# One transformer layer on one core: attention jobs of 4 heads by 256 queries, denominators from pair sums, a 256-token feed-forward, and two PSUM banks shared between matmul groups and attention outputs

## The chip, the cores and the metric

The kernel runs on one core of one Trainium2 chip. The metric is the device time of one execution in microseconds (us); lower is better. A core has these engines: TensorE for matrix products (PE in the profile, with PEld for its weight loads), VectorE (DVE), ScalarE (ACT), GpSimd (POOL), and SyncE (SP), which starts the DMA transfers here. The kernel allocates its tiles on chip, in SBUF, and for what matmuls write one tensor in PSUM, of 8 banks of 128 partitions x 512 float32.

## The reference, cut to what matters

```python
B, S, D, H, F = 1, 2048, 1024, 32, 3584          # bf16; head width 32
def _A_ref(x, wqkv, wo):
    qkv = (x @ wqkv).reshape(B, S, 3, H, 32).transpose(2, 0, 3, 1, 4)
    q, k, v = qkv
    scores = einsum("bhqd,bhkd->bhqk", q, k) * 32 ** -0.5
    p = softmax(scores, axis=-1)
    o = einsum("bhqk,bhkd->bhqd", p, v)
    return o.transpose(0, 2, 1, 3).reshape(B, S, D) @ wo
def _B_ref(x, w1, b1, w2, b2):
    return gelu(x @ w1 + b1, approximate=True) @ w2 + b2     # tanh form
h   = x + _A_ref(layernorm(x), wqkv, wo)
out = h + _B_ref(layernorm(h), w1, b1, w2, b2)
```

The attention makes 32 x 2048 x 2048 exponentials. All of them are on ScalarE, as 1024 instructions of 128 x 1024 elements. The feed-forward has 28 blocks of 128 hidden features.

## The kernel before

The program first builds a list of tasks with their dependences. A list scheduler with fixed cost constants then chooses, at build time, the order of the instructions on each engine. Each engine gets its list in that order, with semaphore waits between the engines. So a change can move work between stages without any line saying so.

An attention job of before is 2 heads x 512 queries. Scores use 32-row tiles of the array. The products with V, the denominators (a product with ones) and all other matmuls that run during attention use four tiles of 32 columns side by side. I call four such matmuls one *step*.

```python
def mm(bank, lhsT, rhs, start, stop, reads, narrow, cols=(0, 512)):     # all other matmuls
    c0, c1 = cols
    if narrow:                                                           # during attention
        for j in range(4):
            ... p.matmul(psum[32*j:32*j+32, bank, c0:c1], lhsT[:, 32*j:32*j+32], rhs,
                         start=start, stop=stop, tile_position=(0, 32*j), ...)
        pe(fns, occ, reads=reads, writes=[B_ps[bank]], mode="col")
    else:                                                                # in the tail
        pe(lambda p: p.matmul(psum[:, bank, c0:c1], lhsT, rhs, ...), ..., mode="full")

# Att.qk: per unit, 2 score matmuls of 512 columns and one exponential of 128 x 1024
act(lambda a: a.activation(PT[:, s, :, :], psum[:, 2*u:2*u+2, :], ACT.Exp, bias=0.0, scale=SCALE), 1024, ...)

# Att.pv_unit: one step holds both the products with V and the denominators of one unit
for j in range(2):
    ... p.matmul(psum[32*j:32*j+32, bank, :], V[:, kt, 32*h:32*h+32], PT[:, s, j, :],
                 tile_position=(0, 32*j), ...)
for j in range(2):
    ... p.matmul(psum[64+32*j:96+32*j, bank, :], ones32[:, :], PT[:, s, j, :],
                 tile_position=(0, 64+32*j), ...)

# Att.finish: copies of 64 x 512 out of PSUM, then per pair of jobs four of these, and a product
v.reciprocal(Dsb[:, 128*k:128*k+128], Dsb[:, 128*k:128*k+128])
```

PSUM banks 0 to 5 hold scores. Bank 6 belongs to the attention outputs and bank 7 to all other matmul groups. With one bank, the next group waits until VectorE has emptied the bank: in the run before_again below, matmuls waited 35 times, 11.3 us in all, for the VectorE additions of the feed-forward that do this (waits view). The feed-forward of 512 tokens runs under the attention of the next 512 tokens. The last 512 tokens have no attention left to hide behind; that part is the *tail*, and it may use all eight banks.

The softmax here doesn't subtract the row's maximum and nothing guards it: scores larger than these inputs give would overflow.

Of the kernel before, what the change touches and what calls it, by code (L numbers as in the profile page):

```python
# [12 lines left out]
P = 128  # L13
# [14 lines left out]
class Task:  # L28
    __slots__ = ("eng", "fns", "occ", "lat", "deps", "prio", "kind", "mode", "left", "succ", "ready", "done",
                 "order", "inc", "flow", "value", "lane", "waits", "bytes", "hold")  # L30

    def __init__(self, eng, fns, occ, lat, prio, kind, mode):
        self.eng, self.fns, self.occ, self.lat = eng, fns, occ, lat
        self.prio, self.kind, self.mode = prio, kind, mode
        self.deps = set()
        self.succ = []
        self.left = 0
        self.ready = 0.0
        self.done = None
        self.order = None  # L40
        self.inc = False
        self.flow = None
        self.value = 0
        self.lane = None
        self.waits = ()
        self.bytes = 0
        self.hold = None


class Graph:  # L50
# [47 lines left out]
    def schedule(self, pick_pe, switch=0.1, dma_rate=280.0, dma_lat=2.1, dma_issue=0.06):  # L98
        for i, t in enumerate(self.tasks):
            t.left = len(t.deps)  # L100
            for d in t.deps:
                d.succ.append(t)
        ready = {e: [] for e in self.ENGS}
# [18 lines left out]
        while n < total:  # L122
# [5 lines left out]
            for e in self.ENGS:  # L128
                while free[e] <= now + 1e-9:
# [41 lines left out]
                    n += 1  # L171
                    for s in t.succ:
                        s.left -= 1
                        if s.left == 0:
                            release(s)
# [109 lines left out]
def build_kernel(nc, A_x, A_wqkv, A_wo, B_w1, B_b1, B_w2, B_b2, out):  # L285
# [5 lines left out]
    NCH = S // 512  # L291
# [13 lines left out]

    BASE, TOP = 16512, 229344

    class Area:
        def __init__(self, start):
            self.cur = start  # L310

        def take(self, shape, dtype, align=64):
# [6 lines left out]
            assert self.cur <= TOP, (shape, self.cur - TOP)  # L319
# [3 lines left out]


# [26 lines left out]
    att_lo = top.cur  # L351
    KT2, B_KT = sb(top, "KT2", [P, 16, 4, 2, P], BF, 64, 2)
    V, B_V = sb(top, "V", [P, NT, D], BF, 4 * NT)
    att_hi = top.cur
    NQ = 4
    QT2, B_QT = sb(top, "QT2", [P, NQ, 2, 512], BF, NQ)
    NPT = 7
    PT, B_PT = sb(top, "PT", [P, NPT, 2, 512], BF, NPT)
    ot_lo = Area(top.cur)
    OT, B_OT_ = sb(top, "OT", [P, 2, G, 512], BF, 2 * G, 4)  # L360
    B_OT = [B_OT_[:G], B_OT_[G:]]
    xrb, B_xrb = sb(ot_lo, "xrb", [P, 8, D], BF, 8)
    Osb, B_Osb = sb(top, "Osb", [P, 512], F32, parts=2)
    Dsb, B_Dsb_ = sb(top, "Dsb", [P, 512], F32, parts=8)
    B_Dsb = [B_Dsb_[:4], B_Dsb_[4:]]
    ph0 = Area(top.cur)
    ffn = Area(top.cur)


    xnT, B_xnTt = sb(ph0, "xnT", [P, 4, DC, 512], BF, 4, 4)  # L370
    Wall, B_W = sb(ph0, "Wall", [P, 6, DC, 512], BF, 6, 4)
    NXB = 4
    xb, B_xb = sb(ph0, "xb", [P, NXB, D], BF, NXB)
    NSG = 2
    stg, B_stg = sb(ph0, "stg", [P, NSG, 512], BF, NSG)


    hch, B_hch = sb(ffn, "hch", [P, 4, D], BF, 4)
    gT, B_gT = sb(ffn, "gT", [P, FC, 512], BF, FC)

    class Rings:


        def __init__(self, area, pfx, nw1, nw2, ngl, nos, nx, nxb):
            self.nw1, self.nw2, self.ngl, self.nos, self.nx, self.nxb = nw1, nw2, ngl, nos, nx, nxb
            self.cnt = {"w1": 0, "w2": 0, "x": 0, "xb": 0, "gl": 0, "os": 0}
            self.x, self.B_x = sb(area, pfx + "xr3", [P, self.nx, 512], BF, self.nx)
            self.w1, self.B_w1 = sb(area, pfx + "w1r", [P, nw1, DC, 256], BF, nw1)
            w2_area = Area(area.cur + 3 * 4096)
            self.w2, self.B_w2 = sb(area, pfx + "w2r", [P, nw2, 4, 512], BF, nw2)  # L390

            if nw2 == 7:
                self.xq, self.B_xq = sb(w2_area, pfx + "xq", [P, DC, 512], BF)
                self.hnT, self.B_hnT = sb(w2_area, pfx + "hnT", [P, DC, 512], BF, 1, 4)
            self.xb, self.B_xb = sb(area, pfx + "xb3", [P, self.nxb, D], BF, self.nxb)
            self.xh, self.B_xh = sb(area, pfx + "xh", [P, ngl, 512], BF, ngl)
            self.sq, self.B_sq = sb(area, pfx + "sq", [P, ngl, 512], BF, ngl)
            self.uu, self.B_uu = sb(area, pfx + "uu", [P, ngl, 512], BF, ngl)
            self.th, self.B_th = sb(area, pfx + "th", [P, ngl, 512], F32, ngl)
            self.ost, self.B_ost = sb(area, pfx + "ost", [P, nos, 512], BF, nos)  # L400

        def next(self, k, n):
            i = self.cnt[k] % n
            self.cnt[k] += 1
            return i

    R1 = Rings(ffn, "a_", 4, 7, 2, 2, 2, 2)
# [4 lines left out]

    qd = nc.dram_tensor("q_scratch", [G, NCH, P, 512], BF, kind="Internal").ap()
    xd = nc.dram_tensor("x_scratch", [3, P, DC, 512], BF, kind="Internal").ap()
    B_xd = [gr.buf() for _ in range(3)]
    B_qd = [[gr.buf() for _ in range(NCH)] for _ in range(G)]


    MM = 0.2195
    def c_dve_ps(n):  # L420
        return (120 + n) / 960.0 + 0.02
# [10 lines left out]
    def mm(bank, lhsT, rhs, start, stop, reads, narrow, cols=(0, 512)):  # L432

        c0, c1 = cols
        occ = MM * (c1 - c0) / 512.0 + 0.003
        if narrow:
            fns = []
            for j in range(4):
                fns.append(lambda p, j=j: p.matmul(psum[32 * j:32 * j + 32, bank, c0:c1], lhsT[:, 32 * j:32 * j + 32], rhs,  # L439
                                                   start=start, stop=stop, tile_position=(0, 32 * j), skip_group_check=True))  # L440
            pe(fns, occ, reads=reads, writes=[B_ps[bank]], mode="col")
        else:
            pe(lambda p: p.matmul(psum[:, bank, c0:c1], lhsT, rhs, start=start, stop=stop),  # L443
               occ, reads=reads, writes=[B_ps[bank]], mode="full")
# [18 lines left out]

# [10 lines left out]


    cnt = {"ln": 0, "x": 0, "sg": 0, "pt": 0}

    def layer_norm(tiles, prio, norm="dve"):

# [20 lines left out]
        for k, (x_ap, B_x, o_ap, B_o) in enumerate(tiles):  # L500
            eng, cost = (dve, 0.58) if norm == "dve" else (pool, 3.8)
            eng(lambda e, k=k, x_ap=x_ap, o_ap=o_ap: e.tensor_scalar(
                o_ap, x_ap, mvr[:, i + k, :], rden[:, i + k, :], ALU.subtract, ALU.mult), cost,
                reads=[B_x, B_mvr[i + k], B_rden[i + k]], writes=[B_o], prio=prio)

    def transposes(src_ap, B_src, bank, dst_ap, B_dst, evac, prio):
        for dc in range(DC):
            pe(lambda p, dc=dc: p.transpose(psb[:, bank, dc * P:(dc + 1) * P], src_ap[:, dc * P:(dc + 1) * P], ident[:]),  # L508
               0.064, reads=[B_src, B_ident], writes=[B_ps[bank]], prio=prio)
        src = psb[:, bank, :].rearrange("p (dc t) -> p dc t", dc=DC)  # L510
        if evac == "act":
            act(lambda a: a.activation(dst_ap, src, ACT.Copy), 1024, reads=[B_ps[bank]], writes=[B_dst], prio=-1)  # L512
        else:
            dve(lambda v: v.tensor_copy(dst_ap, src), c_dve_ps(1024), reads=[B_ps[bank]], writes=[B_dst])


    def load_w(blk, prio, c0=0, c1=512, after=()):
        dma(Wall[:, blk, :, c0:c1], A_wqkv[:, blk * 512 + c0:blk * 512 + c1].rearrange("(dc p) c -> p dc c", p=P),
            P * DC * (c1 - c0) * 2, writes=B_W[blk][c0 // P:c1 // P], prio=prio, after=after)

    def x_slot(tt):
        return xrb[:, tt % 8, :], B_xrb[tt % 8]
# [5 lines left out]
    def ln_tiles(tts, prio, norm):  # L528
        layer_norm([x_slot(tt) + (xb[:, tt % NXB, :], B_xb[tt % NXB]) for tt in tts], prio, norm)

    def tr_tile(tt, bank, evac, prio=0):
        tc, t4 = divmod(tt, 4)
        transposes(xb[:, tt % NXB, :], B_xb[tt % NXB], bank, xnT[:, tc, :, t4 * P:(t4 + 1) * P], B_xnTt[tc][t4], evac, prio)

    def proj(which, g, tc, bank, evac, direct=False):

        blk, c = divmod(which * D + g * P, 512)
        for dc in range(DC):
            mm(bank, Wall[:, blk, dc, c:c + P], xnT[:, tc, dc, :], dc == 0, dc == DC - 1,
               [B_W[blk][c // P]] + B_xnTt[tc], True)  # L540
        s = cnt["sg"] % NSG
        cnt["sg"] += 1
        if evac == "act":
            act(lambda a: a.activation(stg[:, s, :], psum[:, bank, :], ACT.Copy), 512,
                reads=[B_ps[bank]], writes=[B_stg[s]], prio=-1)
        else:
            dve(lambda v: v.tensor_copy(stg[:, s, :], psum[:, bank, :]), c_dve_ps(512), reads=[B_ps[bank]], writes=[B_stg[s]])  # L547
        if which == 1:
            for pr in range(2):
                for half in range(2):  # L550
                    dve(lambda v, pr=pr, half=half: v.tensor_copy(
                        KT2[64 * half:64 * half + 64, 2 * g + pr, tc, :, :],
                        stg[64 * pr:64 * pr + 64, s, 256 * half:256 * half + 256]), c_dve(256, 4),
                        reads=[B_stg[s]], writes=[B_KT[4 * (2 * g + pr) + tc][half]])
        else:
            if direct:
                for pr in range(2):
# [449 lines left out]
```

## Time and profile before

The timed runs took 1204.71 us (median; 1203.74 to 1205.07). The first profiled execution took 1417.9 us. The page of that profile, its first rows: busy time with share of the span and instruction count per engine; the granted TensorE clock in 40 slices, in tenths of full speed; the shares of the chain of work that ended last; and two groups of instructions (busy us, mean ns | idle time before them and what ended it).

```profile
span 1417.9 us, 37847 instructions
PE 1366.2 (96%) x17326; PEld 510.9 (36%) x17336; DVE 673.2 (47%) x1165; ACT 1085.3 (77%) x1189; POOL 37.9 (3%) x96
PEclk7777777777777777777777777777777777766777
PE 91%; ACT 4%; DVE 3%; issue 1%; POOL 1%; DMA 0%; POOLq 0%; DVEq 0%
L643 ACT ACTIVATE PT<-ps 128x1024 bf16<-128x1024 f32 x1024 | 989.2, 1025 | 180.5 <-PE ps L634 166.1
L673 DVE RECIPROCAL Dsb<-Dsb 128x128 f32<-128x128 f32 x128 | 115.1, 928 | 1.0
```

This page looks like a kernel bound by TensorE, but the clock row is 6 to 7 from end to end (0.749 in the mean), and the span is 18% longer than the timed runs. It is a page taken at a lower clock. There is a second run of the kernel before (label before_again, 1204.6 us). The same parts of its page, with two rows on DMA (all packets; and queue q8, which carries instructions: packets, MB, share of the engines' time):

```profile
span 1202.8 us, 37857 instructions
PE 1130.1 (94%) x17336; PEld 465.1 (39%) x17336; DVE 668.8 (56%) x1165; ACT 1059.9 (88%) x1189; POOL 38.2 (3%) x96
PEclk9999999999999999999999999999999999978999
DMA packets 165793, 112.29 MB, mean 93 GB/s; under 512 B 25345, under 2 KB 162817, under 8 KB 164866
q8 instruction: 136, 2.23, 0.8%
L643 ACT ACTIVATE PT<-ps 128x1024 bf16<-128x1024 f32 x1024 | 967.6, 1034 | 33.5 <-PE ps L634 20.1
```

And the view of windows for 100 us in the middle of attention (busy us and count of PE, PEld, DVE, ACT, POOL; clock; DMA share; GB/s):

```profile
500.00:600.00 100.00, 95.88 (x1528) 36.11 (x1520) 42.91 (x65) 99.16 (x107) 4.60 (x12) 1.00 0.35 110
```

| kernel before, at full clock | us |
|---|---|
| start to the first exponential | 23.3 |
| first to last exponential ("attention") | 1050.8 |
| of that, ScalarE idle | 34.9 |
| tail, after the last exponential | 128.7 |

### The profile page before, as it was taken

Reading aid. Unit: us, or ns where it says so; the run is one execution under the profiler, and the core shown is the slowest. Engines: PE = TensorE matmul, PEld = TensorE weight load, DVE = VectorE, ACT = ScalarE, POOL = GpSimd, SP = SyncE. Lnnn points to the kernel's source line nnn. Section 1 sums busy time; section 2 is a strip of 40 time slices with the busy share of each in tenths; the row PEclk is TensorE's granted clock in tenths of the full one; section 3 lists DMA queues with packets and bytes.
Section 4 is the critical chain, followed back from the end, with each engine's and each line's share of the span. In section 5 each row is a group of like instructions: output and inputs, shape, how many; then the busy total and the mean of one; then the engine's idle time right before and its main releaser. Section 6 shows DMA issues by size and latency. Waiting matters only on the chain.

```text
span 1417.9 us, 37847 instructions
## 1 busy us (share of the span) xinstructions
PE 1366.2 (96%) x17326; PEld 510.9 (36%) x17336; DVE 673.2 (47%) x1165; ACT 1085.3 (77%) x1189; POOL 37.9 (3%) x96
## 2 busy tenths in 40 slices
PE   8999999999999999999999999999999999978999
PEld 5544443433333333332333333333333333324333
DVE  7354444443546774223547762225677612245710
ACT  4778787878888888888888888888988888844500
POOL 2000000000100000000100000000000000001000
PEclk7777777777777777777777777777777777766777
DMA  6800000025343222303342230422323322202222
GB/s 165 224 2 13 28 13 14 13 72 156 101 122 101 76 69 72 124 16 98 107 124 71 83 98 16 124 71 63 107 73 98 102 66 85 87 0 75 74 93 71
DMA packets 165793, 112.29 MB, mean 79 GB/s; under 512 B 25345, under 2 KB 162817, under 8 KB 164866
## 3 DMA queue, kind: packets, MB, share of 16 engines
q1 hardware_dynamic: 165634, 109.87, 26.2%
q8 instruction: 136, 2.23, 0.7%
q14 instruction: 23, 0.19, 0.1%
HBM read 98.58 MB, written 11.27 MB: 77 GB/s over the span
## 4 chain that ended last, share of the span: by engine, by line
PE 91%; ACT 4%; DVE 3%; issue 1%; POOL 1%; DMA 0%; POOLq 0%; DVEq 0%
PE ps L439 48%; PE ps L654 17%; PE ps L634 12%; PE ps L443 10%; ACT PT L643 3%; PE ps L658 2%; PE ps L798 1%; ACT xnT L512 1%; DVE a_xh L748 1%; PE ps L508 1%; DVE V L606 0%; DVE stg L547 0%; DVE Osb L668 0%; DVE Dsb L666 0%; DMA a_w1r<-in_A_wqkv_dram 0%
## 5 line engine op out<-in xcount | busy, mean ns | idle before, releaser
L643 ACT ACTIVATE PT<-ps 128x1024 bf16<-128x1024 f32 x1024 | 989.2, 1025 | 180.5 <-PE ps L634 166.1
L654 PE MATMUL ps<-PT,V 128*32 128x512 bf16 x2048 | 383.4, 457 | 13.7 <-DVE V L606 6.2
L658 PE MATMUL ps<-PT,ones 128*32 128x512 bf16 x2048 | 384.8, 458 | 0.0
L439 PE MATMUL ps<-a_w2r,gT 128*32 128x512 bf16 x2688 | 241.9, 452 | 0.0
L634 PE MATMUL ps<-QT,KT 32*128 32x512 bf16 x2048 | 216.7, 414 | 7.4 <-ACT PT L643 7.3
L439 PE MATMUL ps<-a_hnT,a_w1r 128*32 128x512 bf16 x2688 | 215.2, 454 | 4.0 <-DVE a_xh L748 3.2
L654 PEld LDWEIGHTS ps<-PT,V 128*32 128x32 bf16 x2048 | 103.3, 104 | 143.9 <-issue 89.3
L634 PEld LDWEIGHTS ps<-QT,KT 32*128 32x128 bf16 x2048 | 51.5, 91 | 272.3 <-ACT PT L643 164.5
L439 PE MATMUL ps<-xnT,Wall 128*32 128x512 bf16 x1344 | 111.6, 453 | 7.0 <-ACT xnT L512 4.8
L439 PEld LDWEIGHTS ps<-a_w2r,gT 128*32 128x32 bf16 x2688 | 77.3, 109 | 112.0 <-issue 103.3
L673 DVE RECIPROCAL Dsb<-Dsb 128x128 f32<-128x128 f32 x128 | 115.1, 928 | 1.0
L439 PEld LDWEIGHTS ps<-a_hnT,a_w1r 128*32 128x32 bf16 x2688 | 70.6, 107 | 108.0 <-issue 71.4
L782 DVE SCALAR_TENSOR_TENSOR a_ost<-ps,hch 128x512 bf16<-128x512 f32 x24 | 16.6, 692 | 189.8 <-PE ps L439 189.7
L658 PEld LDWEIGHTS ps<-PT,ones 128*32 128x32 bf16 x2048 | 103.5, 104 | 6.6 <-issue 6.6
L748 DVE TENSOR_SCALAR a_xh<-ps,b1f 128x512 bf16<-128x512 f32 x84 | 63.1, 751 | 81.3 <-PE ps L439 80.2
L666 DVE COPY Dsb<-ps 64x512 f32<-64x512 f32 x64 | 44.4, 694 | 101.5 <-PE ps L658 100.1
L439 PE MATMUL ps<-Wall,xnT 128*32 128x256 bf16 x2048 | 83.8, 314 | 0.0
L547 DVE CAST stg<-ps 128x512 bf16<-128x512 f32 x40 | 27.5, 689 | 89.2 <-PE ps L439 89.2
L443 PE MATMUL ps<-a_hnT,b_w1r 128*128 128x512 bf16 x219 | 64.5, 470 | 2.1 <-ACT a_hnT L512 1.5
L439 PEld LDWEIGHTS ps<-Wall,xnT 128*32 128x32 bf16 x2048 | 57.6, 107 | 22.7 <-issue 11.3
L443 PE MATMUL ps<-a_w2r,gT 128*128 128x512 bf16 x219 | 64.1, 461 | 0.5
L439 PE MATMUL ps<-a_w1r,OT 128*32 128x512 bf16 x768 | 63.1, 453 | 0.8 <-DVE hch L719 0.5
(69 smaller groups left out, 875.5 us busy)
## 6 DMA issues: line engine op xcount, KB each, us to landing
a_w2r<-in_B_w_dram SPq DMA_DIRECT2D x56, 512.0 KB, 4.6
a_w1r<-in_B_w_dram SPq DMA_DIRECT2D x42, 512.0 KB, 3.9
a_w1r<-in_A_wo_dram SPq DMA_DIRECT2D x16, 512.0 KB, 4.7
QT<-q_scratch SPq DMA_DIRECT2D x60, 128.0 KB, 2.8
b_w1r<-in_B_w_dram SPq DMA_DIRECT2D x14, 512.0 KB, 3.8
a_w1r<-in_A_wqkv_dram SPq DMA_DIRECT2D x11, 512.0 KB, 5.1
xrb<-in_A_x_dram SPq DMA_DIRECT2D x16, 256.0 KB, 3.9
Wall<-in_A_wqkv_dram SPq DMA_DIRECT2D x16, 256.0 KB, 5.4
```

The source lines that it names most:

```text
L439: fns.append(lambda p, j=j: p.matmul(psum[32 * j:32 * j + 32, bank, c0:c1], lhsT[:, 32 * j:32 * j + 32], rhs, start=start, stop=stop, tile ...
L443: pe(lambda p: p.matmul(psum[:, bank, c0:c1], lhsT, rhs, start=start, stop=stop), occ, reads=reads, writes=[B_ps[bank]], mode="full")
L508: pe(lambda p, dc=dc: p.transpose(psb[:, bank, dc * P:(dc + 1) * P], src_ap[:, dc * P:(dc + 1) * P], ident[:]), 0.064, reads=[B_src, B_ide ...
L547: dve(lambda v: v.tensor_copy(stg[:, s, :], psum[:, bank, :]), c_dve_ps(512), reads=[B_ps[bank]], writes=[B_stg[s]])
L634: return p.matmul(psum[:, 2 * u + j, :], KT2[r0:r0 + 32, p16, tc, i, :], QT2[r0:r0 + 32, qs, pr, :], start=True, stop=True, tile_position= ...
L643: act(lambda a, u=u, s=s: a.activation(PT[:, s, :, :], psum[:, 2 * u:2 * u + 2, :], ACT.Exp, bias=0.0, scale=SCALE), 1024, reads=[B_ps[2 * ...
L654: fns.append(lambda p, j=j, h=h: p.matmul(psum[32 * j:32 * j + 32, bank, :], V[:, kt, 32 * h:32 * h + 32], PT[:, s, j, :], start=first, st ...
L658: fns.append(lambda p, j=j: p.matmul(psum[64 + 32 * j:96 + 32 * j, bank, :], ones32[:, :], PT[:, s, j, :], start=first, stop=last, tile_po ...
L666: dve(lambda v: v.tensor_copy(Dsb[64 * pr:64 * pr + 64, :], psum[64:128, bank, :]), c_dve_ps(512), reads=[B_ps[bank]], writes=B_Dsb[pr], p ...
L673: dve(lambda v, k=k: v.reciprocal(Dsb[:, 128 * k:128 * k + 128], Dsb[:, 128 * k:128 * k + 128]), 0.93, reads=[B_Dsb[0][k], B_Dsb[1][k]], w ...
L748: dve(lambda v, i=i, fc=fc, bank=bank: v.tensor_scalar(R.xh[:, i, :], psum[:, bank, :], b1f[:, fc:fc + 1], None, ALU.add), c_dve_ps(512), ...
L782: dve(lambda v, o=o, t4=t4, j=j, bank=bank: v.scalar_tensor_tensor(R.ost[:, o, :], psum[:, bank, :], 0.5, hch[:, t4, 512 * j:512 * j + 512 ...
```

## The change

The intent: fewer TensorE steps for the attention outputs, short reciprocals, a tail half as large, and no waiting for one PSUM bank.

- A job is 4 heads x 256 queries. Its products with V fill four column tiles of 256 columns. For the denominators VectorE first adds two blocks of exponentials (496 *pair sums*, all but the first two jobs), so the product with ones is needed on half the data.
- The denominators are transposed in blocks of 32 x 32, so 8 reciprocals per partition replace 128 (0.928 us).
- wo, the second layer norm and the feed-forward run in chunks of 256 tokens. Weights are read from memory eight times instead of four. All these matmuls, now in the tail too, are four column tiles of 256 columns.
- Banks 6 and 7 form a pool. The scheduler gives a free one to the next matmul group or the next job.

The core of the diff:

```diff
-    def mm(bank, lhsT, rhs, start, stop, reads, narrow, cols=(0, 512)):
+    def mm(g, lhsT, rhs, start, stop, reads, cols=(0, 512)):
         c0, c1 = cols
+        fns = []
+        for j in range(4):
+            fns.append(lambda p, j=j: p.matmul(psum[32 * j:32 * j + 32, g.bank, c0:c1], lhsT[:, 32 * j:32 * j + 32], rhs, ...))
+        grp_pe(g, fns, occ, reads, "col")
...
+    class Job:                                   # 4 heads x 256 queries; 8 rounds
+        def round(self):
...                                               # 8 score matmuls of 256 columns, 2 exponentials of 128 x 1024
+            if not self.direct:
+                dve(lambda v: v.tensor_tensor(PS[:, z, :, :], PT[:, s, :, 0:256], PT[:, s, :, 256:512], ALU.add), ...)
+            for i in range(2):
+                for hh in range(4):
+                    ... p.matmul(psum[32*hh:32*hh+32, self.bank, 0:256], V[:, g, 2*r+i, 32*hh:32*hh+32],
+                                 PT[:, s, hh, 256*i:256*i+256], tile_position=(0, 32*hh), ...)
+        def den(self, r, s):
+            srcs = [PT[:, s, :, 0:256], PT[:, s, :, 256:512]] if self.direct else [PS[:, s, :, :]]
...                                               # ones32 times each source: 4 matmuls of 256 columns
+        def finish(self):
+            v.transpose(DT[:, f, :], psum[:, self.bank, 256:512])
+            v.tensor_copy(OS[:, f, :], psum[:, self.bank, 0:256])
+            v.reciprocal(RB[:, f, :], ...)        # 8 elements per partition
+            v.transpose(RT[:, f, :], ...)
+            v.tensor_tensor(OT[:, c % NOT, g, :], OS[:, f, :], RT[:, f, :], ALU.mult)
...
     def pick_pe(rd, now, state, up):             # qk first, then pv, then the rest, as before
+        free = [b for b, ts in pool_of.items() if all(x.done is not None and x.done <= now + 1e-9 for x in ts)]
...
+            if t.grp.bank is None:                # a group takes a free bank when it starts
+                b = free[0]
+                t.grp.bank = b
+                t.deps.update(pool_of[b])
+                pool_of[b] = t.grp.buf.r
```

The static order holds 4488 steps before and 4240 after (counted in units of 512 columns), of which 525 and 383.5 follow the last scores. The number of matmul instructions rises from 17,336 to 32,304.

## The prediction

> **What bounds the kernel now.** The profiled execution took 1417.9 us, the timed ones 1204.7. The granted clock in the profile is 0.75 from 17 us on (page row PEclk). Back-to-back 512-column matmul steps (four 32-column tiles count as one) start 0.285 us apart[...]. The instruction order holds 4488 such steps: 4488 x 0.285 = 1278 us, more than the timed runs took. So the timed runs had a faster clock, and the profile's "PE 96%" is no proof for them.[...]
>
> ScalarE: 18 consecutive exponentials take 16.60 us, one per 0.916. 1024 of them, 84 tanh at about 0.53 and 16 copies need about 1000 us, all before the tail. The tail (after the last exponential at 1255 us, timeline) has no attention: 525 steps, 163 us profiled, an estimated 125 at full clock. Start 25 + tail 125 leaves 1055 us for attention; ScalarE needs 1000 of it[...]. Main reading (60%): ScalarE bounds, at full clock. Rival (40%): a clock near 0.87, TensorE bounds as in the profile.
>
> **What the change does.**
> - TensorE: PV and denominators fall from 1024 steps to about 512 + 256. Total 4488 to 4240, -5.5%. Matmuls rise from 17,300 to 32,300, most now 256 columns; in the trace 256-column steps go at 0.145 us, so halving the width costs 1 to 2% at this clock.
> - VectorE: adds 496 pair sums of 128x1024 bf16 (the 128x512 square took 0.42 us[...], so about 0.69 each, 340 us) and 64 finishes of five short operations, about 120 us. Removes reciprocals (115 us), half-bank copies (88), staging shuffles (about 60). 673 to about 920 us, over 80% of the span: a near-bound.
> - ScalarE: 98 tanh instead of 84 under attention, +7 us.
> - Tail: by the order listing 383 steps follow the last scores instead of 525: -30 us of matmul, about -5 of waits.
> - Between two score groups: 6.6 steps before, 6.4 after, but 8.6 and 7.7 in the first two sixteenths (projections), where TensorE is the slower.
>
> So most of the saved steps pay for tail work moved under attention.
>
> **Sum.** If ScalarE bounds: 1205 - 35 (tail) + 7 (tanh) + 10 (early projections) - 10 (fewer one-bank stalls) = 1177. If TensorE bounds: 1205 x 0.945 = 1138. Weighted, with some credit for pooled banks: **1158 us**, range 1105 to 1195. Chances: 0.70 / 0.24 / 0.06 (faster, same, slower).
>
> **What would show it.** Tail after the last exponential a quarter shorter (timeline). If the profile after is at 0.75 again, its span falls to about 1340, TensorE still over 90% in the chain, ScalarE's idle before exponentials under 180 us. Pair sums 0.65 to 0.72 us, VectorE at least 65% of the profiled span. TensorE's waits for VectorE evacuations under 40 us. Undoing the pair sums alone should cost under 2% if ScalarE bounds, about 5% if TensorE does.
>
> **What would make it wrong.** VectorE delaying evacuations, so that two pooled banks starve TensorE (1200 or more). 256-column steps limited by weight loads or issue at full clock[...]. Or one-bank stalls being the true loss of before: then pooling gains more, down to 1100.

The sum came to 1205 - 35 + 7 + 10 - 10 = 1177 if ScalarE bounds and 1205 x 0.945 = 1138 if TensorE does, weighted to 1158. What it says of full clock is the author's estimate; the first profile's own figures give nearly the same: 163 us x 0.75 = 122 for the tail (125 in the text), 142 fewer steps x 0.285 us x 0.75 = 30. The 0.69 us of a pair sum is an estimate (measured later: 0.684 us, and 0.420 us for half of it in a1_halfsum). The clock of that profile was 0.75 from 5.4 us on, not from 17, but for two stretches at 0.5.

## The result, and the profile after

The changed kernel took 1217.01 us (median of 4; 1213.38 to 1223.95), the kernel before 1204.24 us in the same rounds. The ratio is 1.0115 with a 95% interval of 1.0083 to 1.0146. Ratios here are the mean time of one kernel's fast runs over that of the other's fast runs in the same rounds, so they are not quite the ratio of the medians quoted. The change made the kernel 1% slower; the predicted range ended at 1195.

The page after, the rows that answer to those of before:

```profile
span 1214.9 us, 68329 instructions
PE 1107.3 (91%) x32304; PEld 775.5 (64%) x32304; DVE 836.0 (69%) x1575; ACT 1053.0 (87%) x1183; POOL 34.7 (3%) x80
PEclk9999999988999999999999999999999999998999
DMA packets 332265, 170.06 MB, mean 140 GB/s; under 512 B 26321, under 2 KB 329425, under 8 KB 331986
q8 instruction: 252, 4.13, 1.4%
PE 73%; ACT 16%; DVE 7%; issue 4%; POOL 0%; DVEq 0%; POOLq 0%; ACTq 0%
L676 ACT ACTIVATE PT<-ps 128x1024 bf16<-128x1024 f32 x1024 | 974.4, 1033 | 66.9 <-PE ps L668 53.3
L681 DVE TENSOR_TENSOR PS<-PT 128x1024 bf16<-128x1024 bf16 x496 | 328.8, 684 | 96.0 <-PE ps L705 56.4
```

The window of 500 to 600 us after:

```profile
500.00:600.00 100.00, 92.72 (x2844) 66.89 (x2844) 71.94 (x136) 93.65 (x105) 2.70 (x4) 1.00 0.59 171
```

ScalarE fell from 99.16 to 93.65 us busy in this window. TensorE did not rise in its place: it fell too, from 95.88 to 92.72. Neither engine is saturated, and the clock is 1.00. The stages, from the times of the first and last exponential in each trace:

| stage, us | before (before_again) | after | difference |
|---|---|---|---|
| to the first exponential | 23.3 | 18.9 | -4.3 |
| attention | 1050.8 | 1090.7 | +39.9 |
| of that, ScalarE idle | 34.9 | 63.1 | +28.2 |
| tail | 128.7 | 105.3 | -23.4 |

(Differences are from unrounded times.) Of the +39.9 us in attention, 28.2 is new idle time of ScalarE and 7.3 is 14 more tanh of 0.524 us; the other 4.4 us were not broken down.

The waits view after says what ScalarE and TensorE waited for (us in total, times, longest; "issue" is waiting for nothing that the profile shows):

```profile
PEld ps L668 <- ACT PT L676: 58.2, 151, 1.2
ACT PT L676 <- PE ps L668: 53.3, 71, 4.3
PE ps L493 <- issue: 26.8, 38, 1.8
PE ps L493 <- DVE a_xh L780: 17.8, 29, 1.4
```

ScalarE waits for scores (L668). L493 is the common matmul helper. It waits 38 times for "issue", 0.7 us each on average. One case from the timeline of TensorE (start, us, then the group; the bracket is idle time before it); "128*32 128x256" is a stationary tile of 128 x 32 and a moving tile of 128 x 256:

```profile
323.22 1.48 PE L493 MATMUL ps<-hnT,wr 128*32 128x256 bf16 x46
326.45 0.29 PE L493 MATMUL ps<-hnT,wr 128*32 128x256 bf16 x2 [1.75 <-issue]
326.46 0.50 PE L686 MATMUL ps<-PT,V 128*32 128x256 bf16 x8
326.89 0.40 PE L668 MATMUL ps<-QT,KT 32*128 32x256 bf16 x8
```

And ScalarE at the same time:

```profile
322.95 1.94 ACT L676 ACTIVATE PT<-ps 128x1024 bf16<-128x1024 f32 x2
327.34 3.77 ACT L676 ACTIVATE PT<-ps 128x1024 bf16<-128x1024 f32 x4 [2.45 <-PE ps L668]
```

TensorE stops in the middle of one matmul group for 1.75 us and waits for nothing that the profile shows. The scores queued behind it come late, and ScalarE has nothing to do for 2.45 us. In the tail, where nothing else mixes in, the places of such stops form a pattern. TensorE's timeline in the tail:

```profile
1134.90 1.59 PE L493 MATMUL ps<-wr,gT 128*32 128x256 bf16 x49 [1.02 <-issue]
1136.23 0.49 PE L493 MATMUL ps<-b2t,two_row 128*32 128x256 bf16 x8
1136.45 2.13 PE L493 MATMUL ps<-wr,gT 128*32 128x256 bf16 x71
1139.74 3.68 PE L493 MATMUL ps<-wr,gT 128*32 128x256 bf16 x128 [1.16 <-issue]
1144.59 0.94 PE L493 MATMUL ps<-wr,gT 128*32 128x256 bf16 x25 [1.17 <-issue]
1145.26 0.49 PE L493 MATMUL ps<-b2t,two_row 128*32 128x256 bf16 x8
```

From one stop to the next there are 49 + 8 + 71 = 128 matmuls, then 128 again. Each matmul comes with one weight load (32,304 of each on the page), so this is every 256 TensorE instructions. Counted over the whole trace after, TensorE stops for more than 0.3 us on "issue" 38 times in attention (28.7 us) and 12 times in the tail (13.4 us). (A stop is measured from the start of one matmul to the start of the next, less the 0.109 us of a step.) When TensorE's instructions are numbered, its few semaphore waits included, all 50 stops fall on the same place of a block of 256, give or take one instruction; the counts of the experiments below include up to three pauses elsewhere. The kernel before (before_again) has no such stop at that place.

The instruction queue fits this. From before to after it grows by 252 - 136 = 116 packets, and TensorE's instructions grow by 2 x (32,304 - 17,336) = 29,936. That is one packet per 258 instructions; 4.13 MB / 252 is 16.4 KB per packet. The author reads this so: TensorE stops where a new block of its own program has to come in. The times of the packets agree. The trace has one q8 packet for each block end, in order; at each of the 50 stops TensorE went on between 1.2 and 1.6 us after that block's packet had landed. At the block ends without a stop the packet had landed a median 2.4 us before. A block of 128 matmuls, as 32 steps, takes 32 x 0.216 = 6.9 us with steps of 512 columns, and 32 x 0.109 = 3.5 us with steps of 256.

### The profile page after: what moved, and what is told of

Same layout as the page of the kernel before. It is cut to its first block, busy times and chain, and to the rows that moved or that the text cites. A ratio compares the mean times of both kernels' runs of the same rounds, so it can differ in the third digit from the quotient of the medians.

```text
span 1214.9 us, 68329 instructions
## 1 busy us (share of the span) xinstructions
PE 1107.3 (91%) x32304; PEld 775.5 (64%) x32304; DVE 836.0 (69%) x1575; ACT 1053.0 (87%) x1183; POOL 34.7 (3%) x80
## 3 DMA queue, kind: packets, MB, share of 16 engines
q8 instruction: 252, 4.13, 1.4%
## 4 chain that ended last, share of the span: by engine, by line
PE 73%; ACT 16%; DVE 7%; issue 4%; POOL 0%; DVEq 0%; POOLq 0%; ACTq 0%
PE ps L493 50%; ACT PT L676 14%; PE ps L668 11%; PE ps L686 7%; PE ps L705 4%; DVE PS L681 2%; ACT a_th L786 1%; DVE a_xh L780 1%; PE ps L823 1%; DVE hch L745 1%; DVE a_sq L784 1%; PE ps L555 1%; ACT xnT L558 0%; DVE gT L788 0%; DVE DT L714 0%
## 5 line engine op out<-in xcount | busy, mean ns | idle before, releaser
L681 DVE TENSOR_TENSOR PS<-PT 128x1024 bf16<-128x1024 bf16 x496 | 328.8, 684 | 96.0 <-PE ps L705 56.4
L493 PE MATMUL ps<-hnT,wr 128*32 128x256 bf16 x6272 | 224.7, 276 | 22.5 <-DVE a_xh L780 11.4
L493 PE MATMUL ps<-wr,gT 128*32 128x256 bf16 x6608 | 224.1, 274 | 11.0 <-issue 10.6
L668 PE MATMUL ps<-QT,KT 32*128 32x256 bf16 x4096 | 207.0, 275 | 16.7 <-ACT PT L676 14.1
L686 PE MATMUL ps<-PT,V 128*32 128x256 bf16 x4096 | 193.0, 277 | 20.8 <-ACT PT L676 15.0
L493 PEld LDWEIGHTS ps<-hnT,wr 128*32 128x32 bf16 x6272 | 157.8, 97 | 62.3 <-issue 45.2
L493 PEld LDWEIGHTS ps<-wr,gT 128*32 128x32 bf16 x6608 | 168.0, 97 | 42.2 <-issue 37.0
L705 PE MATMUL ps<-PS,ones 128*32 128x256 bf16 x1984 | 145.9, 279 | 4.8 <-DVE PS L681 3.4
L668 PEld LDWEIGHTS ps<-QT,KT 32*128 32x128 bf16 x4096 | 61.6, 92 | 135.7 <-issue 71.4
L686 PEld LDWEIGHTS ps<-PT,V 128*32 128x32 bf16 x4096 | 101.3, 97 | 50.7 <-ACT PT L676 26.6
L493 PE MATMUL ps<-xnT,Wall 128*32 128x512 bf16 (+1 forms) x1952 | 106.4, 340 | 3.7 <-ACT xnT L558 1.1
L493 PE MATMUL ps<-wr,OT 128*32 128x256 bf16 x2048 | 77.3, 284 | 6.3 <-DVE hch L745 4.1
L493 PEld LDWEIGHTS ps<-xnT,Wall 128*32 128x32 bf16 x1952 | 48.1, 98 | 36.2 <-issue 11.4
L493 PE MATMUL ps<-Wall,xnT 128*32 128x256 bf16 x2048 | 67.7, 273 | 0.9 <-ACT xnT L558 0.7
L493 PEld LDWEIGHTS ps<-wr,OT 128*32 128x32 bf16 x2048 | 53.3, 100 | 20.3 <-issue 13.2
```

The lines of the kernel that those rows point to most:

```text
L493: fns.append(lambda p, j=j: p.matmul(psum[32 * j:32 * j + 32, g.bank, c0:c1], lhsT[:, 32 * j:32 * j + 32], rhs, start=start, stop=stop, ti ...
L668: fns.append(lambda p, i=i, hh=hh, r0=r0: p.matmul(psum[:, 2 * us[hh // 2] + hh % 2, 256 * i:256 * i + 256], KT[r0:r0 + 32, g, 256 * r + P ...
L681: dve(lambda v: v.tensor_tensor(PS[:, z, :, :], PT[:, s, :, 0:256], PT[:, s, :, 256:512], ALU.add), c_dve(1024, 2), reads=B_PT[s], writes= ...
L686: fns.append(lambda p, i=i, hh=hh: p.matmul(psum[32 * hh:32 * hh + 32, self.bank, 0:256], V[:, g, 2 * r + i, 32 * hh:32 * hh + 32], PT[:, ...
L705: fns.append(lambda p, i=i, hh=hh, src=src: p.matmul(psum[32 * hh:32 * hh + 32, self.bank, 256:512], ones32[:, :], src[:, hh, :], start=False,
```

## The experiments

Theory A, the main rival before the runs: VectorE, busy 69%, delivers pair sums and emptied banks late. Theory B: TensorE's instructions do not come fast enough; the half-wide matmuls double their number, and the doubled weight traffic competes for DMA. Further suspects were the pooled banks and the first V projections. All labels but before_again are timed; ratios are against the kernel before in the same rounds, and the changed kernel's is 1.0115.

### 1. before_again: the kernel before, unchanged

Edit: none.

> The kernel before, unchanged, profiled once more. Its first profile was taken at a granted clock of 0.75 and a span of 1418 us, although its timed runs took 1204 us. If the timed runs had the full clock, this profile now shows a clock above 0.95, a span near 1200 us, a tail after the last exponential near 125 us, and ScalarE as the engine without slack (idle between exponentials under 70 us in the attention stage). If the timed runs had a clock near 0.87, the profile shows that. If it falls at 0.75 again, the comparison of the two traces has to be made by counts alone.

Measured: 1204.6 us, clock 0.989 in the profile; see above. The timed runs have the full clock, and ScalarE bounds the kernel before. The first profile was of another state of the clock (0.749).

### 2. e1_direct: the changed kernel without pair sums

```diff
-        def __init__(self, g, c, bank=None, direct=False):
+        def __init__(self, g, c, bank=None, direct=True):
```

> The kernel after, but with the denominators of all jobs from the exponentials themselves on TensorE, as its first two jobs have them: 496 pair sums (329 us of VectorE) go, 496 more 256-column steps (0.109 us each, 54 us of TensorE, 1984 more matmuls) come. Theory A, VectorE's load is what eats the gain (late evacuations of the two banks, late pair sums): faster than the kernel after, 1180 us or less. Theory B, TensorE is the engine that has no slack left (its idle in the attention stage is short stalls, not missing work): slower by about 54 us, 1260 to 1275. Theory C, ScalarE alone bounds and TensorE has room: within 1% of 1217.

Measured: 1236.84 us, ratio 1.0284 (1.0249 to 1.0319), 1.7% above the changed kernel. VectorE fell to 44% of the span, and yet ScalarE's idle time in attention rose to 82.7 us. TensorE made 34,288 matmuls; its stops at block ends rose to 63 in attention (49.8 us). Relieving VectorE did not help, so Theory A falls as the main cause. The time lies outside all three expected ranges (their Theory B is TensorE without slack, not B above): the extra steps are 54 us of TensorE work, but the kernel lost only 19.8 us. The stops grew by 21.1 us in attention and fell from 13.4 to 8.9 in the tail; a growth of that size fits B.

### 3. c1_split: the kernel before, each 512-column matmul as two of 256

Same order of tasks, same work, same data; only the number of matmuls changes. The score matmuls stay at 512 columns.

```diff
-    for j in range(4):
-        ... p.matmul(psum[32*j:32*j+32, bank, c0:c1], lhsT[:, 32*j:32*j+32], rhs, ...)
+    for o in (0, 256):
+        for j in range(4):
+            ... p.matmul(psum[32*j:32*j+32, bank, o:o+256], lhsT[:, 32*j:32*j+32], rhs[:, o:o+256], ...)
```

(and the same in pv_unit)

> The kernel before, in its own instruction order, with every 512-column matmul of its background groups and of PV and denominators issued as two of 256 columns: the same TensorE work (a 256-column step took 0.109 us, a 512-column one 0.216), the same VectorE, ScalarE and DMA work, but 29,700 matmuls instead of 17,300. Theory I, instruction supply (TensorE stands still at multiples of 128 matmuls, that is of 256 of its instructions, when these last only 3.5 us): such stalls of over 0.3 us, of which the kernel before had none, appear, and the time rises by 15 to 45 us to 1218 to 1248. Rival, the width itself costs nothing and the stalls come from the new program's DMA traffic or buffers: within 8 us of 1203.

Measured: 1230.49 us, ratio 1.0241 (1.0226 to 1.0257). The page and the waits show 232 instruction packets and, on the matmul helper (L445 here), issue waits; the waits view of before_again has no such row for its matmuls:

```profile
PE 1143.5 (93%) x29710; PEld 784.6 (64%) x29720; DVE 669.3 (55%) x1165; ACT 1063.5 (87%) x1189; POOL 37.9 (3%) x96
q8 instruction: 232, 3.80, 1.3%
PE ps L445 <- issue: 11.2, 13, 1.5
```

Attention took 1075.8 us with 57.0 us of ScalarE idle time, against 1050.8 and 34.9. There were 15 stops at block ends, 15.9 us; nine more pauses on "issue", of 0.4 to 0.5 us, lay elsewhere (3.9 us). The number of TensorE instructions alone makes the kernel before 2.4% slower. This is the cleanest test of the half of B that blames the instruction count: no other part of the change is in it.

### 4. t1_tailfull: the changed kernel, whole-array matmuls in the tail

```diff
     def mm(g, lhsT, rhs, start, stop, reads, cols=(0, 512)):
         c0, c1 = cols
+        if g.name.startswith((f"f2.{NC - 2}", f"wo{NC - 1}", f"f1.{NC - 1}", f"f2.{NC - 1}")):
+            grp_pe(g, lambda p: p.matmul(psum[:, g.bank, c0:c1], lhsT, rhs, ...), occ, reads, "full")
+            return
```

> The kernel after, with the matmuls of the stage without attention (last output projection, last two feed-forward halves) on the whole array: one matmul instead of four column tiles, so a quarter of the instructions there. Theory I: the 12 stalls of the tail (13 us) go, tail 105 to about 92 us, time about 1204. Rival (the tail waits for weight DMA or for VectorE): tail stays at 105 us. A third result, slower, would say that loading 128 columns of weights does not hide behind 256 columns of data.

Measured: 1196.15 us, ratio 0.9951 (0.9936 to 0.9966). The tail fell from 105.3 to 90.6 us, with no stop at a block end. TensorE's timeline in its tail, where one matmul of 128 x 128 weights replaces four of 128 x 32:

```profile
1122.57 6.28 PE L493 MATMUL ps<-wr,gT 128*128 128x256 bf16 x56
1128.68 0.38 PE L493 MATMUL ps<-b2t,two_row 128*128 128x256 bf16 x2
1128.90 6.28 PE L493 MATMUL ps<-wr,gT 128*128 128x256 bf16 x56
```

58 matmuls start within 6.33 us (1122.57 to 1128.90), 0.109 us each: the step has the same cadence with a quarter of the instructions. Attention, where nothing was edited, still stopped 33 times (27.2 us). 90.6 is 38.1 us below the tail of before; the prediction had -35.

### 5. f1_full: the changed kernel, every such matmul whole-array

The same edit with the condition `if True:`.

> The kernel after, with all projection and feed-forward matmuls on the whole array: 16,100 matmuls instead of 32,300, at the price of more changes between array modes (0.1 us each as measured at score matmuls). Theory I: no stall over 0.3 us at multiples of 128 matmuls is left, ScalarE's idle time that follows such stalls (28 of 63 us) is gone, and if the mode changes cost under 0.1 us for every other boundary the time is 1165 to 1200; if mode changes eat it, 1200 to 1240 without stalls at block ends. Rival (stalls are not instruction supply): stalls stay.

Measured: 1180.82 us, ratio 0.9823 (0.9809 to 0.9838); 16,056 matmuls by the order, 126 instruction packets. No stop at a block end was left. Attention took 1041.9 us with 27.0 us of ScalarE idle time, of which 10.1 is one gap at 101 us (experiment 8). The tail grew to 118.0 us: the scheduler counts a change of the array's mode as 0.1 us (in the trace after two steps of 256 columns start a median 0.208 us apart where the mode changes from scores to column tiles, 0.215 us the other way and 0.215 us from column tiles to the whole array, against 0.109 to 0.120 us without a change), every switch between a job's column tiles and a whole-array group is now one, and so it left 474 steps for the tail in place of 383.5. This run removes the stops at another price.

### 6. d1_halfdma: the changed kernel, half of the weight bytes (wrong result)

The instruction order is the same; once a ring slot has been filled, later loads bring half of it.

```diff
-        dma(w, src_ap.rearrange("(dc p) c -> p dc c", p=P), P * n * 512, writes=[b], prio=1)
+        k = n // 2 if id(b) in loaded else n
+        if n == 8:
+            loaded.add(id(b))
+        dma(w[:, 0:k, :], src_ap.rearrange("(dc p) c -> p dc c", p=P)[:, 0:k, :], P * n * 512, writes=[b], prio=1)
```

> Wrong result on purpose: the kernel after in the same instruction order, but each weight block after the first into a buffer brings only half of its bytes (the other half is what lay there before). DMA traffic falls from 170 MB to under 110 MB, about that of the kernel before. If the instruction stalls come from DMA traffic in the way of instruction fetches, they shrink from 42 us to under 15 and the time falls by 20 to 40 us. If they come from the rate of instructions alone, stalls and time stay (1205 to 1222).

Measured: 1175.63 us, ratio 0.9779 (0.9759 to 0.9799).

```profile
DMA packets 203241, 104.00 MB, mean 89 GB/s; under 512 B 26321, under 2 KB 200401, under 8 KB 202962
q8 instruction: 252, 4.13, 1.4%
ACT PT L676 <- PE ps L668: 24.4, 36, 4.3
PE ps L493 <- issue: 3.7, 10, 1.1
```

With the same 252 instruction packets, the stops fell from 38 to 10 in attention (5.2 us; two of them, 1.1 us, lie away from block ends) and from 12 to 4 in the tail (1.7 us). ScalarE's idle time fell from 63.1 to 33.6 us. So the stops depend on the rate of fetches and on the other DMA traffic together. The waits view of the changed kernel shows no wait of a matmul for a weight transfer, so the gain here is not weights that arrive earlier. With c1_split (114 MB, near before's 112, but more instructions: 16 us of stops at block ends) and f1_full (168 MB, but few instructions: none) both factors have been varied alone.

### 7. p1_onebank: the changed kernel without the pool

During attention, jobs get bank 6 alone and matmul groups bank 7 alone.

```diff
-        new_ok = len(free) > 1 or (free and (not idle_job or not pv_ready or (waiting <= PV_START - 2 and not last)))
+        free_job = [b for b in free if b == 6 or last]
+        free = [b for b in free if b != 6 or last]
+        new_ok = bool(free)
```

> The kernel after with the pooling of the two PSUM banks undone: attention outputs get bank 6 alone, background groups bank 7 alone, until the last scores are out. The scheduler then finds less room for background work under attention: 580 steps of 512 columns stay behind the last scores instead of 383. If the pooled banks are worth what the change hoped, this is slower than the kernel after by about 197 x 0.216 = 43 us of tail less what attention gets faster, 1235 to 1265, with the waits of TensorE for VectorE evacuations above 60 us (57 us before, 48 after in steps over 0.15 us). If pooling is worth nothing, within 1% of 1217.

Measured: 1256.17 us, ratio 1.0455 (1.0438 to 1.0472). Without the pool, 580 steps are left for the tail, which takes 162.7 us. Pooling is worth about 3.4% (1.0455 against 1.0115), some 40 us: it is what moves work of the tail under attention. Waits of matmuls for VectorE, summed over the rows of PE in the waits view, were 78.7 us, against 33.6 with the pool and 38.1 in before_again. Attention itself took 1072.8 us here, less than the 1090.7 of the changed kernel, with 197 more steps left for the tail. Pooling does not cause the loss.

### 8. v1_vsplit: the changed kernel, V projections spread out

The changed kernel has an 8.54 us gap on ScalarE at 102 us:

```profile
110.61 7.60 ACT L676 ACTIVATE PT<-ps 128x1024 bf16<-128x1024 f32 x8 [8.54 <-PE ps L686]
```

L686 is the product with V. The author's reading: all buffers of exponentials are full, their products need V, and V's projection for two head groups is done in one piece. The edit gives each of two jobs half of it.

```diff
-        if g % 2 == 0:
-            for tt in range(0, NT, 2):
-                proj_v(group(f"pv{g}.{tt}"), tt, g // 2, "dve")
+        if g < 7:
+            q, h = divmod(g + 1, 2)
+            for tt in range(8 * h, 8 * h + 8, 2):
+                proj_v(group(f"pv{g}.{tt}"), tt, q, "dve")
```

> The kernel after, with the V projections of each pair of head groups spread over the two groups before they are needed, as the kernel before had them. In the kernel after ScalarE stands still for 8.5 us at 102 us, because all its eight buffers of exponentials wait for V columns that are projected in one piece. If that is the cause, the gap goes and the time falls by 5 to 10 us to 1207 to 1212; stalls at instruction block ends stay (35 to 45 us).

Measured: 1203.27 us (1201.60 to 1216.17), ratio 1.0049 (0.9992 to 1.0106). The gap moved rather than went. ScalarE's timeline:

```profile
93.45 14.93 ACT L676 ACTIVATE PT<-ps 128x1024 bf16<-128x1024 f32 x16 [7.67 <-PE ps L668]
```

The run also had fewer stops in attention (34, 23.4 us), by luck of the order, and one execution was as slow as the changed kernel. What the edit itself is worth stays unclear here.

### 9. a1_halfsum: the changed kernel, half of each pair sum (wrong result)

The pair sums cover two of four heads, at 0.420 us in place of 0.684; the order of matmuls is as before. A memset at the start fills the rest of the sum buffer with ones.

```diff
-                dve(lambda v: v.tensor_tensor(PS[:, z, :, :], PT[:, s, :, 0:256], PT[:, s, :, 256:512], ALU.add), ...)
+                dve(lambda v: v.tensor_tensor(PS[:, z, 0:2, :], PT[:, s, 0:2, 0:256], PT[:, s, 0:2, 256:512], ALU.add), ...)
```

> Wrong result on purpose: the kernel after in the same instruction order, each pair sum over two of the four heads only (the rest of the sum buffer is set to one at the start). A pair sum then takes about 0.42 instead of 0.68 us, so VectorE loses about 130 us of work and nothing else changes. Theory A (VectorE's load delays evacuations and pair sums): 15 us or more faster, under 1202. Theory I (instruction supply): within 8 us of 1217, stalls at block ends as many as before.

Measured: 1207.09 us (1202.32 to 1210.54), ratio 1.0043 (1.0007 to 1.0078). VectorE's busy time fell from 836 to 722.5 us. ScalarE's idle time did not fall (63.9 against 63.1), nor did the stops (39 in attention, 34.1 us). The ratio is 0.7% below the changed kernel's for 114 us less work on VectorE, and the intervals barely separate. The time missed both expected ranges (under 1202; 1209 to 1225). The result is small and not clear.

### 10. h1_mixed: v1_vsplit, with the form of each matmul chosen by what precedes it

The scheduler emits a background matmul as four column tiles only where TensorE already stands in that mode and attention outputs are still to come, and whole-array elsewhere. That leaves few added changes of mode: 1220 in the trace, against 1080 in the changed kernel and 1607 in f1_full.

```diff
+        one = [lambda p: p.matmul(psum[:, g.bank, c0:c1], lhsT, rhs, ...)]
-        grp_pe(g, fns, occ, reads, "col")
+        grp_pe(g, fns, occ, reads, "col").alt = {"col": fns, "full": one}
...
+            if t.alt:                            # in pick_pe, as the task is chosen
+                t.mode = "col" if state["mode"] == "col" and n < len(pvs) else "full"
+                t.fns = t.alt[t.mode]
```

> A candidate to beat both: the kernel after with V spread as in v1_vsplit, and each background matmul on the whole array (one instruction) wherever TensorE does not come from PV or denominators, so the only extra mode changes are from whole-array matmuls to PV: 19,400 matmuls instead of 32,300, tail again 383 steps. Theory I: stalls at block ends under 10 us in all, tail near 92 us, attention near 1045 us, time 1145 to 1172. If the whole-array matmuls in attention cost more than they save, above 1180.

Measured: 1159.87 us, ratio 0.9653 (0.9639 to 0.9668). 19,410 matmuls, 152 instruction packets, 168 MB of DMA. One stop of 0.5 us is left. Attention took 1047.9 us, the tail 91.7 us with the same 383.5 steps as the changed kernel. Compared with v1_vsplit, the edit changes only the form of the matmuls, though the scheduler's order changes with it: 43 us less. The stops of that run measured 23.4 + 10.1 = 33.5 us; what the remaining 10 us are was not separated.

### 11. h2_order: h1_mixed with both query halves of a head group in succession

```diff
-    order = [(1, 0), (2, 0)]
-    for g in range(1, 6):
-        order += [(g, 1), (g + 2, 0)]
-    order += [(6, 1), (7, 1)]
+    order = [(g, c) for g in range(1, 8) for c in range(2)]
```

> h1_mixed with the first attention jobs taken two by two of one head group, (1,0) (1,1) (2,0) and so on, instead of (1,0) (2,0) (1,1): a head group's projections then have 16 rounds of attention to hide behind instead of 8. In h1_mixed ScalarE stands still for 7.2 us at 87 us, because the next group's Q and K come behind V in TensorE's order; the longest run of background work between two score groups falls from 39 steps to 20. Expected: that gap gone, 1150 to 1157. If it only moves again, 1158 to 1162.

Measured: 1145.91 us (1144.49 to 1147.60), ratio 0.9534 (0.9518 to 0.9550). It beats both kernels. Two jobs now follow each projection, so the next one has 16 rounds of attention to hide behind in place of 8; the gap near 90 us is gone. The granted clock was also at 0.5 for only 3.4 us, against 23.9 us in h1_mixed, so not all of the 14 us need come from that gap. Its page, its window of 500 to 600 us, and its wait of ScalarE for scores:

```profile
PE 1084.1 (95%) x19380; PEld 720.1 (63%) x19398; DVE 836.2 (73%) x1575; ACT 1046.1 (91%) x1183; POOL 34.2 (3%) x80
q8 instruction: 152, 2.49, 0.9%
```

```profile
500.00:600.00 100.00, 95.92 (x1810) 63.98 (x1810) 77.14 (x145) 99.38 (x113) 0.00 (x0) 1.00 0.59 170
```

```profile
ACT PT L678 <- PE ps L670: 18.6, 22, 4.4
```

ScalarE is back at 99% with the DMA rate of the changed kernel (170 GB/s in this window, 171 there) and with VectorE busier than there (77.14 against 71.94). Attention took 1036.8 us, ScalarE idle 18.4, the tail 91.1.

### 12. h3_direct: h1_mixed without pair sums

The edit of experiment 2, on h1_mixed.

> h1_mixed without the pair sums (denominators of all jobs on TensorE, as e1_direct did to the kernel after): what the pair sums are worth once instruction supply is out of the way. TensorE gets 248 steps of 512 columns more (54 us), VectorE loses 339 us. In the kernel after, undoing them cost 1.6%. If ScalarE bounds the attention stage (98% busy) and TensorE still has slack, under 1.5% slower than h1_mixed, at most 1177. If TensorE has none left, 1195 to 1215, that is the whole 40 to 54 us.

Measured: 1162.09 us, ratio 0.9671 (0.9657 to 0.9686), against 0.9653 (0.9639 to 0.9668) with pair sums. TensorE is 97% busy and VectorE 46%. Without the stops the pair sums are worth 0.2%, and the intervals overlap: the steps they save on TensorE are not what bounds the kernel. In experiment 2 the same edit cost 1.7%; there the further matmuls came with 21.1 us more stops in attention.

All twelve kernels gave correct results but the two that were wrong on purpose.

## Why the prediction was wrong, point by point

**Right: the first profile was not of the timed machine, and ScalarE bounds.** The argument from 4488 steps x 0.285 us held: at full clock steps of 512 columns start 0.216 us apart in the traces, so 4488 of them are 969 us. ScalarE was 99% busy in the middle of attention. The rival reading (clock near 0.87, TensorE bound) is out.

**Right: the direct costs.** Pair sums took 0.684 us (predicted 0.65 to 0.72). VectorE was busy 69% of the span (at least 65), though its 836 us stayed below the estimate of 920 and 80%. Fourteen tanh cost 7.3 us (7). Waits of matmuls for VectorE sum to about 34 us in the waits view (under 40); the count by steps that the expectation of p1_onebank quotes has 48, so this item hangs on the way of counting. Undoing the pair sums cost 1.7% (under 2), though experiment 12, with 0.2% for the same edit where there are no stops, says that most of that was stops and not steps.

**Wrong, and the step that failed: "halving the width costs 1 to 2% at this clock".** The cadence itself lost nothing: steps of 256 columns started 0.109 us apart, half of 0.216. The prediction took the cadence inside runs of matmuls as the whole cost. The sum had no term for bringing in twice as many instructions, with DMA traffic 112 to 170 MB beside it. That term measured 28.7 us of TensorE stops in attention and 13.4 in the tail. Attention grew by 39.9 us where the prediction's terms of attention (+7 tanh, +10 early projections, -10 fewer bank stalls) gave +7. When ScalarE's idle gaps are sorted by the largest delay of TensorE in the 2.5 us before each, 28.2 of the 63.1 us follow such a stop; that sorting is attribution, but c1_split, d1_halfdma and f1_full each show it by removing or adding the stops.

**Near, but the wrong mechanism: "256-column steps limited by weight loads or issue at full clock".** The prediction named issue as a risk, but as a uniform slowing of each step. The steps ran at 0.109 us, and the loss came in stops of 0.3 to 2 us at the ends of blocks of 256 instructions. The instruction queue's row, 136 packets on the page before, was there to be read, and the rise to some 32,300 matmuls was in the prediction itself.

**Mis-sized: the tail, -35 us.** It was -23.4. The steps were right (383.5 against 525), and t1_tailfull, the same tail without stops, measured -38.1. The missing part was stops again.

**Not seen by itself: "10 (fewer one-bank stalls)".** Pooling does what it was meant to (p1_onebank: some 40 us worse without it). From before to after the waits of matmuls for VectorE fell by 4.5 us in the waits view (38.1 to 33.6) and by 9 in the count of the p1_onebank expectation (57 to 48), so a saving of that order is there; what it was worth to attention was not measured apart from the stops and the 8.54 us gap of ScalarE at 102 us, which is the size of the early-projection cost that the prediction put at 10 us.

**Not tested: a span of 1340 us at clock 0.75.** The profile after had the full clock. What the change does at 0.75 stays open.

Without the stops, the changed schedule takes 1160 to 1176 us (h1_mixed, which also holds the spread V projections; d1_halfdma). That is where the prediction's range between its weighted 1158 and its ScalarE sum of 1177 lay. With t1_tailfull this fits a sum with one term absent; the terms of +10 and -10 were not measured one by one, and d1_halfdma still had 6.9 us of stops.

**What stays open.** Why a fetch comes late is narrowed down, not shown. The median fetch took about 0.96 us in its transfer, and fetches were 8.0 us apart in the median before and 4.5 us after, so the average rate is not exhausted. The trace after shows that the transfer itself is not what is slow: it took a median 0.95 us at the 50 stops and 0.96 elsewhere. What is late is its start: a median 2.4 us into the block before at the stops, 1.0 elsewhere. The DMA engines were 82% busy in the waits of over 1.5 us for that start (47 of the 50 stops are among them) and 22% in those under 0.5 us (no stop). This fits fetches that wait for busy DMA engines, as d1_halfdma does; a request that is itself made late is not excluded. What VectorE's load costs stays unclear (a1_halfsum: 0.7% at 114 us less). The granted clock also fell to 0.5 in 7 stretches of 41 us in all, but the kernel before has 27 us of them too, and only one of the 7 (3.4 us) follows a stop at a block end; before the other six TensorE was waiting in short gaps, mostly for ScalarE (matmuls were busy 43 to 65% of the 3.4 us before each of the seven). What these stretches cost was not separated.

## What to carry to other kernels

When a change splits matmuls into narrower ones, count the instructions as well as the column time, read the instruction queue's row of the page, and look for stops on "issue" that come at a fixed distance, 256 TensorE instructions here. Where the array is not already in a column-tiled mode, one whole-array matmul did the same step in a quarter of the instructions (0.109 us either way in t1_tailfull); choosing the form by the preceding mode, with the V projections spread, turned a 1% loss into a 3.5% gain here, and a better job order into 4.7%. And before reading which engine bounds, check the clock row: the first profile named the wrong one.
